# A transformer block with multi-query attention: another order of units, loads and evictions at the start of the kernel

## The chip, the cores and the metric

The kernel runs on one core of a Trainium2 chip, in one launch. The metric is device time in microseconds (us), from an execution of the whole program; lower is better. A core has TensorE (matmuls, written PE in the profile; its weight loads are PEld), VectorE (DVE), ScalarE (ACT), GpSimd (POOL) and SyncE (SP), which here issues nearly all DMAs. Each engine works through its own instructions in order and waits on semaphores for the others.

## The reference

The input x has 2048 tokens of 1024 elements. A condition vector c gives six vectors of 1024 (shift, scale and gate for attention; the same for the FFN). Queries have 32 heads of 32 elements; all heads share one key and one value head.

```python
mod = (silu(c) @ w_mod).reshape(1, 6, 1, -1)
sa, ca, ga, sb, cb, gb = mod[:, 0], ..., mod[:, 5]
h = layernorm(x) * (1 + ca) + sa
q = (h @ wq) -> 32 heads of 32;  k = h @ wk;  v = h @ wv        # one k and v for all heads
p = softmax(q k^T / sqrt(32))
x = x + ga * ((p v) @ wo)
h = layernorm(x) * (1 + cb) + sb
x = x + gb * ((silu(h @ w1) * (h @ w3)) @ w2)                   # F = 3584
```

All matrices are bf16, the output too.

## The kernel before, in words

**Tiling.** The 2048 tokens are eight blocks of 256 (NB, B). A block's attention is eight units of four heads (f = 0 to 7), and a unit goes through eight pairs of key tiles (NJ = 8, 256 keys each). One cycle is one pair of key tiles of one unit: eight S matmuls (K stationary, 32 rows of the array per head, four heads at once) fill four PSUM banks, two exponentials on ScalarE (each 128x1024) write one slot of the ring U, which has NU = 10 slots. After a unit's eight cycles come 64 matmuls with V (four heads at once by columns). The softmax denominator comes from VectorE adding the exponentials (`pairs`, `psum`) and a few matmuls of the sums with ones (`md_own`, or `md` for the later units, which are "merged"). VectorE divides and writes the result over the query tile in QT. In all there are 64 units, 512 cycles and 1024 exponentials.

When the eight units of block n are done, `after_attention(n)` runs: `wo` (output projection for both halves t of 128 tokens, the sum onto x, the second layer norm, and the transposition of the normalized rows to `h2t(n)`: by TensorE for blocks 0 and 7, by DMA for the others), `ffn1` (14 slabs of w1 and w3, each loaded by DMA) and `ffn2` (four quarters of w2). These matmuls (mode F in the code) fill TensorE between the S and V matmuls (modes S and A) of later blocks. After the last exponential only F work remains.

**The start.** SP issues the loads in the order of their due times: x tiles, the w_mod columns of scale (field 1) and shift (field 0), wq in two pieces. Each x tile (tt = 0 to 15) is normalized (`lnt1`: statistics on VectorE, root on GpSimd, the scaled copy on ScalarE for tt < 8 and on VectorE otherwise), transposed by TensorE and evicted to HT by ScalarE or VectorE. The scale is multiplied into wk, wv and wq; the shift enters as a bias: `mod_cols(0)` computes it as 64 narrow matmuls in a bank that it shares with the transposes, SAB holds it, `k_bias` makes the bias of the keys and of two query heads (QKB), `q_bias` that of the others, `v_setup` that of V. `k_proj(j)` makes a pair of key tiles (KT), `q_proj` the queries (QT) and `v_proj` V. The first exponential needs KT of pair 0, QT of unit 0 and so the shift. The queries of blocks 2 to 7 are projected during block 0; wq lies where the FFN's weight slots will be, and HT where the FFN's hidden tiles will be, so both must be done with before the FFN of block 0 can load its weights. `mod_chunk` computes the other four vectors during block 0; the attention gate is multiplied into wo (WOG).

**What sets the order.** Every operation is recorded by `op` with an engine, an estimated duration, the tiles that it reads and writes, and a due time vt. The class `Placer` then replays all of them on its own clock and picks, engine by engine, the next ready operation with the smallest due time plus an offset; S matmuls have by far the smallest due times (TOP). The offsets, and the slacks that say how long an engine may wait for a more urgent operation, stand in `PLAN`, one entry for each eight cycles (SPAN = 8), with an offset for each pair of tag and engine. The result is a fixed order for each engine, with the semaphore waits that it needs. Banks 6 and 7 of PSUM (PB in the profile) are lent to all operations but S; banks 0 to 5 belong to S. An operation with `alts` may go to either of two engines, whichever the planner finds earlier. All instructions are issued from one helper, so the profile has one line number (L22) for them and they are told apart by their tiles.

Names that matter below: `mod_cols` (line 1053), `k_proj` (1121), `v_proj` (1136), `q_proj` (1151), `s_exp` (1214), `sums` (1249), `av` (1312), `wo` (1378), and the loop over units at line 1596.

Of the kernel before, what the change touches and what calls it, by code (L numbers as in the profile page):

```python
# [8 lines left out]
P = 128  # L9
# [33 lines left out]
class Graph:  # L43
# [63 lines left out]
    def alias(self, new, old):  # L107
# [8 lines left out]
    (0.1, 0.03, 0.02, 0, 3.5,  # L116
     {"-/pe": -33, "-/act": 190, "-/dve": 5, "-/pool": 95, "-/sp": 76, "an/dve": -40, "av/dve": -55, "k/dve":
      91, "kb/pe": 35, "ln/pe": -95, "ln/act": 28, "ln/dve": 5, "ln/pool": 1, "mc/pe": 5, "mc/dve": 6, "mc/sp":
      -9, "mod/pe": -73, "mod/dve": 181, "out/sp": -53, "pair/dve": -76, "q/pe": 132, "q/sp": 35, "quarter/pe":
      -104, "quarter/dve": -1, "quarter/sp": 145, "s/pe": -277, "s/act": 37, "sc/dve": -253, "slab/pe": -4,  # L120
      "slab/dve": -34, "slab/sp": 86, "v/pe": 17, "v/dve": 37, "v/pool": 21, "wo/pe": -48, "wo/dve": 4,
      "wo/pool": -43, "wo/sp": -134}),
    (0.15, 0.1, 0.3, 0, 0.4,
     {"-/pe": -22, "-/pool": -69, "-/sp": -59, "an/dve": -5, "av/pe": -93, "av/dve": 169, "k/dve": 28, "kb/pe":
      15, "ln/pe": -116, "ln/dve": -52, "mc/pe": -6, "mc/dve": -14, "mc/sp": -13, "mod/pe": 4, "mod/dve": 88,
      "out/sp": -129, "pair/dve": 109, "q/pe": 17, "q/dve": -175, "quarter/pe": -52, "quarter/dve": 76,
      "quarter/sp": 24, "s/pe": -165, "s/act": -218, "sc/dve": -247, "slab/pe": -51, "slab/act": -199,
      "slab/dve": 23, "slab/sp": 201, "v/pe": -94, "v/dve": -54, "v/pool": 118, "wo/dve": 28, "wo/pool": 3,
      "wo/sp": 81}),
    (0.15, 0.12, 0.3, 1, 0.4,  # L130
     {"-/pe": 14, "-/act": 18, "-/pool": 26, "-/sp": 104, "an/dve": -18, "av/pe": 1, "av/dve": 110, "k/dve":
      118, "ln/pe": -18, "ln/act": 1, "ln/dve": -311, "ln/pool": 109, "mc/pe": 68, "mc/dve": 53, "mc/sp": 12,
      "mod/pe": 78, "out/sp": 258, "pair/dve": -12, "q/pe": 54, "q/dve": -107, "q/sp": -43, "quarter/pe": -71,
# [671 lines left out]
def build(nc, x_in, wq_in, wk_in, wv_in, wo_in, w1_in, w3_in, w2_in, c_in, wmod_in, out, S, D, F):  # L805
# [4 lines left out]
    B = 256  # L810
# [16 lines left out]

# [834 lines left out]
```

## Time and profile before

| | us |
|---|---|
| median of 3 runs | 1135.16 (1134.17 to 1136.1) |
| the profiled execution, time | 1133.24 |
| its span, first to last instruction | 1131.4 |
| ScalarE busy in it | 1019.8 |
| of that, 1024 exponentials | 963.4 |
| VectorE busy | 990.1 |
| mean granted clock of TensorE | 0.995 of full speed |

A row of the stretches gives the stretch, its length, the busy time of each engine with the number of its instructions in brackets, the granted clock, the share of the DMA engines and the GB/s that they moved. A row in order of time gives start, length, engine, operation, output <- input, and how many equal instructions in a row were merged; in square brackets the engine's idle time before it and what ended it. A busy TensorE is not TensorE at its peak: matmuls overlap, and their ends are modelled. "S" as an output is one of the six S banks, "PB" one of the two others; "HT,W" as inputs is a projection or an FFN matmul, "U,V" attention's second product, "PS,ONES" the denominators.

### The profile page before, as it was taken

How to read it: one execution, taken by the hardware profiler on the slowest of the kernel's cores; microseconds unless marked ns; L12 is line 12 of the kernel's file. 1: busy time of each engine (PE TensorE's matmuls, PEld its weight loads, DVE VectorE, ACT ScalarE, POOL GpSimd, SP SyncE). 2: the span in 40 equal slices, each digit the busy share in tenths (PEclk: the TensorE clock that was granted, in tenths of full speed). 3: DMA queues.
4: the chain of work that ended last, by engine and by line, in shares of the span. 5: the costliest groups of instructions: out<-in, count | busy, mean ns of one | idle time of the engine just before them, and what ended most of it. 6: DMA issues, size and time to landing. Idle time of an engine off the chain costs nothing.

```text
span 1131.4 us, 34236 instructions
## 1 busy us (share of the span) xinstructions
PE 1105.2 (98%) x15344; PEld 751.9 (66%) x15376; DVE 990.1 (88%) x1492; ACT 1019.8 (90%) x1161; POOL 55.8 (5%) x95
## 2 busy tenths in 40 slices
PE   8999998999999999999999999999999999999998
PEld 6644445666567766776667766776577757776887
DVE  8989999988899989998899889998999889987542
ACT  6999999999999999999999999999999999984110
POOL 5100000000100001000100001000100001000000
PEclk9999998999999999999999999999999999999999
DMA  9500378655596657965697576775597567677793
GB/s 343 185 2 2 113 205 227 186 169 160 141 248 195 194 146 181 241 196 144 150 270 197 160 192 179 228 197 154 135 264 205 160 174 207 191 220 216 220 295 112
DMA packets 374290, 209.43 MB, mean 185 GB/s; under 512 B 17536, under 2 KB 365952, under 8 KB 374144
## 3 DMA queue, kind: packets, MB, share of 16 engines
q1 hardware_dynamic: 373712, 207.11, 65.8%
q8 instruction: 121, 1.98, 0.8%
q14 instruction: 25, 0.20, 0.1%
q10 hardware_dynamic: 432, 0.13, 0.0%
HBM read 199.89 MB, written 4.19 MB: 180 GB/s over the span
## 4 chain that ended last, share of the span: by engine, by line
ACT 51%; PE 36%; DVE 10%; POOL 1%; issue 1%; POOLq 0%; DVEq 0%
ACT U L22 47%; PE PB L22 23%; PE S L22 13%; ACT HT L22 4%; DVE PS L22 4%; DVE ST L22 2%; DVE X L22 1%; POOL RS L22 1%; DVE QT L22 1%; DVE XNB L22 1%; DVE RB L22 1%; DVE MV L22 0%; DVE HT L22 0%; ACT XNB L22 0%; DVE RC L22 0%
## 5 line engine op out<-in xcount | busy, mean ns | idle before, releaser
L22 ACT ACTIVATE U<-S 128x1024 bf16<-128x1024 f32 x1024 | 963.4, 1170 | 4.6 <-PE S L22 2.6
L22 DVE TENSOR_TENSOR PS<-U 128x2048 bf16<-128x2048 bf16 x256 | 310.2, 1219 | 34.4 <-ACT U L22 31.0
L22 DVE TENSOR_TENSOR PS<-PS 128x1024 bf16<-128x1024 bf16 x312 | 274.5, 882 | 5.0
L22 PE MATMUL PB<-QT,W 128*128 128x256 bf16 x1824 | 228.3, 273 | 1.0
L22 PE MATMUL S<-QT,KT 32*128 32x256 bf16 x4096 | 204.2, 273 | 9.0 <-ACT U L22 5.7
L22 PEld LDWEIGHTS PB<-QT,W 128*128 128x128 bf16 x1824 | 166.4, 98 | 49.8 <-issue 29.2
L22 PE MATMUL PB<-W2S,HT 128*128 128x256 bf16 x1540 | 190.4, 273 | 0.0
L22 PEld LDWEIGHTS PB<-W2S,HT 128*128 128x128 bf16 x1540 | 141.0, 98 | 39.6 <-issue 23.2
L22 PEld LDWEIGHTS S<-QT,KT 32*128 32x128 bf16 x4096 | 60.8, 92 | 139.4 <-ACT U L22 129.7
L22 PE MATMUL PB<-U,V 128*32 128x256 bf16 x4096 | 127.9, 274 | 0.0
L22 PE MATMUL PB<-QT,HT 128*128 128x256 bf16 x928 | 117.8, 273 | 0.7
L22 PEld LDWEIGHTS PB<-U,V 128*32 128x32 bf16 x4096 | 106.5, 97 | 11.1 <-issue 6.1
L22 PE MATMUL PB<-HT,W 128*128 128x256 bf16 (+1 forms) x560 | 98.7, 316 | 3.1 <-issue 2.4
L22 PEld LDWEIGHTS PB<-QT,HT 128*128 128x128 bf16 x928 | 84.8, 98 | 25.4 <-issue 15.1
L22 ACT ACTIVATE HT<-PB 128x512 bf16<-128x512 f32 (+1 forms) x103 | 74.1, 719 | 10.9 <-PE PB L22 10.8
L22 DVE TENSOR_TENSOR HT<-HT,PB 128x512 bf16<-128x512 bf16 x100 | 68.3, 683 | 9.1 <-PE PB L22 7.2
L22 DVE SCALAR_TENSOR_TENSOR HT<-HT,PB 128x512 bf16<-128x512 bf16 x100 | 68.1, 681 | 7.7 <-ACT HT L22 7.1
L22 PEld LDWEIGHTS PB<-HT,W 128*128 128x128 bf16 x576 | 50.0, 97 | 37.0 <-issue 14.9
L22 ACT ACTIVATE HT<-S 128x512 bf16<-128x512 f32 (+1 forms) x16 | 11.1, 702 | 59.9 <-PE S L22 59.9
L22 POOL TENSOR_SCALAR RS<-MV 128x1 f32<-128x1 f32 x32 | 10.5, 327 | 967.9 <-DVE MV L22 966.4
L22 PE MATMUL PB<-WO,QT 128*128 128x512 bf16 x209 | 51.4, 380 | 2.3 <-issue 2.1
L22 PEld LDWEIGHTS PB<-WO,QT 128*128 128x128 bf16 x224 | 18.9, 97 | 25.3 <-issue 6.3
(112 smaller groups left out, 691.8 us busy)
## 6 DMA issues: line engine op xcount, KB each, us to landing
W<-in_B_w_dram SPq DMA_DIRECT2D x150, 512.0 KB, 4.9
W2S<-in_B_w_dram SPq DMA_DIRECT2D x28, 1792.0 KB, 8.5
HT<-in_B_w_dram SPq DMA_DIRECT2D x74, 512.0 KB, 5.0
W2S<-in_w_mod_dram SPq DMA_DIRECT2D x8, 1024.0 KB, 6.9
X<-in_A_x_dram SPq DMA_DIRECT2D x8, 512.0 KB, 6.9
out_dram<-X SPq DMA_DIRECT2D x7, 512.0 KB, 7.8
U<-in_B_w_dram SPq DMA_DIRECT2D x1, 3584.0 KB, 18.2
W2S<-in_B_w_dram SPq DMA_DIRECT2D x1, 3584.0 KB, 13.7
```

What stands on the lines that cost most here:

```text
L22: return getattr(e, call[0])(*call[1], **call[2])
```

## The change

1. Units 0 and 1 (block 0, f = 0 and 1) take turns in halves of the keys: unit 0 with pairs 0 to 3, unit 1 with 0 to 3, unit 0 with 4 to 7, unit 1 with 4 to 7 (`CYC`). After each half, `half` runs V and ones matmuls into one bank, side by side; the first half's bank is copied to PT (f32), the second's added to it. VectorE's `pairs` and `psum` fall away for these two units.
2. The other units of block 0 are two f, that is eight heads, by 128 queries (`UN`): first f 2+3, 4+5, 6+7 with queries 0 to 127, then the same with 128 to 255. QT's dependencies are kept by halves t, and `wo` is split by t; `wo(0, 0)` is recorded after unit 4.
3. The shift's w_mod columns are loaded ahead of x tiles 8 to 11, which become two loads; wq's second piece goes last. `mod_cols(0)` writes to bank 2 instead of a lent bank.
4. Evictions of HT for tiles 10 to 15 and of KT for pairs 2 to 7 have VectorE alone (EVA, EVK). V is projected earlier (VV), and the queries f = 2 to 7 of blocks 0 and 1 are due by pairs.
5. A few estimated durations are changed, and all offsets of `PLAN` are others (66 entries before, 66 after, one of them the same). The instructions of blocks 1 to 7 are the same, their order is not.

```diff
-    (0.1, 0.03, 0.02, 0, 3.5,
-     {"-/pe": -33, "-/act": 190, "-/dve": 5, "-/pool": 95, "-/sp": 76, "an/dve": -40, "av/dve": -55, "k/dve":
...
+    (0.15, 0.06, 0.0, 1, 2.5,
+     {"-/pe": -103, "-/act": -50, "-/sp": 3, "an/dve": 282, "av/dve": -1, "k/pe": -256, "k/dve": -10, "kb/pe":
...
-    LV = {}
+    HALVES = (0, 1)
+    WO00 = 10
+    EVA = 10
+    EVK = 2
+    VV = (-1576, -1575, -1530, -1480)
...
+    PT = [PS[:, k].rearrange("p h q -> p (h q)").bitcast(F32) for k in (1, 3)]
...
-    x_dma(8, 4, -1893)
-    wm_dma(0, 0, -1892)
+    wm_dma(0, 0, -1893)
+    x_dma(8, 2, -1892)
     wm_dma(0, 1, -1891)
-    wq_dma(2, NC, "WQ1", -1890)
+    x_dma(10, 2, -1890)
     x_dma(12, 4, -1889)
+    wq_dma(2, NC, "WQ1", -1888)
...
-        op("act", ev_a, 0.92, reads=bk, writes=hk, vt=vt, sess=s, alts=[("dve", ev_d, 0.6)])
+        if tt < EVA:
+            op("act", ev_a, 0.92, reads=bk, writes=hk, vt=vt, sess=s, alts=[("dve", ev_d, 0.6)])
+        else:
+            op("dve", ev_d, 0.6, reads=bk, writes=hk, vt=vt, sess=s)
 
     def mod_cols(fld):
         G.tag = "mod"
-        s = Sess()
+        s = Sess() if fld else None
+        bk = [] if fld else [("S", 2)]
...
+               writes=[("mod", fld)] + bk, vt=-1800, mode="F", sess=s, post=0.145)
...
+           alts=[] if j >= EVK else [("act", lambda b=0: [lambda e: e.activation(KT[:, ts], BANK[b][:, 0:256], ACT.Identity,
...
+    UN = [(0, f, 1, 0) for f in HALVES] + [(0, f, 2, t) for t in range(2) for f in range(len(HALVES), NC, 2)]
+    UN += [(n, f, 1, 0) for n in range(1, NB) for f in range(NC)]
+    CYC = [(u, q) for a in range(2) for u in HALVES for q in range(4 * a, 4 * a + 4)]
+    CYC += [(u, q) for u in range(len(HALVES), NB * NC) for q in range(NJ)]
+    CIX = {uq: c for c, uq in enumerate(CYC)}
+
+    def qt(u, g=None):
+        n, f, nf, t = UN[u]
+        ps = slice(0, P) if g is None else slice(32 * g, 32 * (g + 1))
+        return QT[ps, n, f:f + nf, t * P:t * P + B // nf]
+
+    def qk(u):
+        n, f, nf, t = UN[u]
+        return [("QT", n, f + k, t + m) for k in range(nf) for m in range(2 // nf)]
+
+    def v3(ap, u):
+        return ap.rearrange("p (a b) -> p a b", a=UN[u][2])
+
...
+    def half(u, a):
+        G.tag = "av"
+        s = Sess(False)
+        t = PT[u]
+        qs = range(4 * a, 4 * a + 4)
+        for q in qs:
+            def mm(b, q=q):
+                return [lambda e, h=h, kk=kk, w=w, c=c: e.matmul(
+                    BANK[b][32 * h:32 * (h + 1), c:c + B], w, U[:, CIX[u, q] % NU, h, kk, :],
+                    start=(q == qs[0] and kk == 0 and c == 0), stop=(q == qs[-1] and kk == 1),
+                    tile_position=(0, 32 * h), skip_group_check=True)
+                    for kk in range(2) for w, c in ((V[:, 2 * q + kk, :], 0), (ONES[:, 0:32], B)) for h in range(4)]
+            op("pe", mm, 0.4368, reads=["ONES", ("V", q // 2), ("U", CIX[u, q] % NU, 0), ("U", CIX[u, q] % NU, 1)],
+               writes=[("av", u)], vt=-500 + u, mode="A", sess=s, post=0.145, after=[exps[(CIX[u, qs[-1]], 1)]])
+        G.tag = "an"
+        if a == 0:
+            op("dve", lambda b: [lambda e: e.tensor_copy(t, BANK[b])], 0.6, reads=[("av", u)], writes=[("PT", u)],
+               vt=u * 8.0, sess=s)
+            return
+        op("dve", lambda b: [lambda e: e.tensor_tensor(t, t, BANK[b], ALU.add)], 0.62, reads=[("av", u), ("PT", u)],
+           writes=[("PT", u)], vt=u * 8.0, sess=s)
+        op("dve", lambda: [lambda e: e.transpose(RB[:, 0, :], t[:, B:2 * B])], 0.37, reads=[("PT", u)],
+           writes=["RBD"], vt=u * 8.0)
+        finish_av(u, t[:, 0:B], ("PT", u))
...
-    def wo(n, vt):
...
+    def wo(n, t, vt):
         G.tag = "wo"
-        for t in range(2):
...
+    def norm2(n, vt):
+        G.tag = "wo"
         if 0 < n < NB - 1:
...
-                o.bw = 200e3
+                o.bw = 185e3
...
-        v_proj(tb, -1150 + tb)
+        v_proj(tb, VV[tb])
...
-        q_proj(0, 2, f, 8.0 * f - 30)
+        q_proj(0, 2, f, 8.0 * (f // 2) - 22)
...
-        wo(n, e0 - 30)
+        for t in range(2):
+            if n or t:
+                wo(n, t, e0 - 30)
+        norm2(n, e0 - 30)
...
-    for u in range(NB * NC):
-        for j in range(NJ):
-            s_exp(NJ * u + j)
+    for c, (u, q) in enumerate(CYC):
+        s_exp(c)
+        if u in HALVES:
+            if q % 4 == 3:
+                half(u, q // 4)
+            if q == 7:
+                G.alias([("PS", (1, 3)[u])], [("PT", u)])
+            continue
+        if q < NJ - 1:
+            continue
         av(u)
-        done = [v for v in ((u - 1, u) if not merged(u) else (u - 1,)) if v % NC == NC - 1 and v >= 0 and
-                (v == u) != merged(v)]
-        for v in done:
-            after_attention(v // NC)
+        if u == 4:
+            wo(0, 0, WO00)
+        if not merged(u) and u % NC == NC - 1:
+            after_attention(u // NC)
+        elif u and merged(u - 1) and u % NC == 0:
+            after_attention(u // NC - 1)
     last = 64 * NB - 1
     later = []
```

More of the change, by code (lines that the diff above doesn't have):

```diff
@@ L1250, in sums @@
         if u < MERGE0:
-            lev = LV.get(u, 2)
-            for q in range(0, NP, 2) if lev else ():
-                pairs(u * NJ + q, q)
+            for q in range(0, NP, 2):
+                pairs(CIX[u, q], q)
                 G.tag = "av"
-                if lev > 1:
-                    psum(q, q, q + 1, u * NJ + q + 102.0)
-            return list(range(0, NP, lev)) if lev else []
+                psum(q, q, q + 1, u * NJ + q + 102.0)
+            return list(range(0, NP, 2))
         acc = 4 + u % 2
@@ L1368, in h2t, with h2k @@
         return H20 if n == 0 else QT[:, n - 1, :, :]
-    def h2k(n):
-        return [("H20", cc) for cc in range(NC)] if n == 0 else [("QT", n - 1, cc) for cc in range(NC)]
+    def h2k(n, cs=range(8)):
+        return [("H20", cc, t) if n == 0 else ("QT", n - 1, cc, t) for cc in cs for t in range(2)]
     def xk(n, t, qs=range(4)):
```

977 lines of the change are left out of this document (491 added, 486 removed).

## The prediction, made before the change was run

> **What bounds the kernel now.** I read the page first (busy shares), then busy time in stretches, then the chain of waits, and last the instructions in order of time where the stretches show idle engines.
>
> ```profile
> span 1131.4 us, 34236 instructions
> PE 1105.2 (98%) x15344; PEld 751.9 (66%) x15376; DVE 990.1 (88%) x1492; ACT 1019.8 (90%) x1161; POOL 55.8 (5%) x95
> ...
> core 0: us, PE busy (x) PEld busy (x) DVE busy (x) ACT busy (x) POOL busy (x), PEclk, DMA share, GB/s
> 0.00:10.00 10.00, 8.46 (x70) 6.27 (x70) 5.26 (x13) 4.08 (x5) 2.98 (x14) 1.00 0.82 286
> 10.00:20.00 10.00, 8.48 (x130) 6.68 (x128) 9.72 (x25) 8.86 (x9) 6.54 (x15) 0.83 1.07 371
> 20.00:30.00 10.00, 7.96 (x156) 6.87 (x154) 9.73 (x23) 5.80 (x6) 6.16 (x15) 0.99 1.06 380
> ...
> 40.00:152.00 112.00, 107.42 (x1627) 52.22 (x1646) 103.44 (x173) 112.00 (x124) 0.79 (x2) 1.00 0.16 50
> 152.00:185.00 33.00, 27.70 (x500) 14.54 (x504) 30.11 (x57) 31.54 (x35) 4.59 (x4) 0.90 0.92 248
> 185.00:1000.00 815.00, 807.32 (x11370) 551.74 (x11380) 755.09 (x1077) 811.60 (x928) 30.59 (x36) 1.00 0.70 189
> ...
> 1040.00:1080.00 40.00, 40.00 (x346) 33.06 (x345) 19.70 (x36) 4.18 (x7) 1.59 (x4) 1.00 0.88 249
> ```
>
> Four stages. Up to 30 us the kernel loads and normalizes x; VectorE is 97% busy from 10 us on, and ScalarE has not begun its exponentials. From 40 to 152 us (attention of block 0) ScalarE is busy all 112 us: it sets the pace. From 152 to 185 us ScalarE goes on, but TensorE has only 27.70 us of 33: it has run out of other work and waits for block 0's second layer norm. From 185 us to 1000 us TensorE (99.1%) and ScalarE (99.6%) are tied, and the tail after 1040 us is TensorE alone at 100%. So the end is TensorE's total work plus its idle time, and nearly all of that lies ahead of 185 us. The change works there.
>
> **Step 1: the exponentials begin sooner.** ScalarE, then TensorE and VectorE, in order of time:
>
> ```profile
> 25.06 1.75 PE L22 MATMUL PB<-SCC,U 128*128 128x16 bf16 x64
> ...
> 27.58 0.14 DVE L22 CAST SAB<-PB 128x8 bf16<-128x8 f32 x1
> ...
> 28.00 0.54 PE L22 MATMUL PB<-SAB,W 128*128 128x16 bf16 x16
> ...
> 29.15 0.10 DVE L22 COPY QKB<-PB 128x3 f32<-128x3 f32 x1
> ...
> 30.29 0.40 PE L22 MATMUL S<-QT,KT 32*128 32x256 bf16 x8
> ```
> ```profile
> 30.76 3.76 ACT L22 ACTIVATE U<-S 128x1024 bf16<-128x1024 f32 x4
> 34.38 0.96 ACT L22 ACTIVATE KT<-PB,QKB 128x256 bf16<-128x256 f32 x2
> 35.39 1.02 ACT L22 ACTIVATE U<-S 128x1024 bf16<-128x1024 f32 x1
> 36.35 0.47 ACT L22 ACTIVATE KT<-PB,QKB 128x256 bf16<-128x256 f32 x1
> 36.73 1.01 ACT L22 ACTIVATE U<-S 128x1024 bf16<-128x1024 f32 x1
> 37.63 0.48 ACT L22 ACTIVATE KT<-PB,QKB 128x256 bf16<-128x256 f32 x1
> 38.11 1.02 ACT L22 ACTIVATE HT<-PB 128x1024 bf16<-128x1024 bf16 x1
> 39.03 31.29 ACT L22 ACTIVATE U<-S 128x1024 bf16<-128x1024 f32 x34
> ```
>
> The first exponential at 30.76 us is the end of a chain from the shift: its 64 narrow matmuls at 25.06, SAB, the biases QKB, keys and queries, S. The three rates of the load stage give (286+371) x 10 = 6.57 MB by 20 us. Queued up to the end of the shift are, by the code, 8 x tiles (2.10 MB), two fields of w_mod (4.19), the first wq columns (0.52), x tiles 8 to 11 (1.05) and wk, wv (0.13): 7.99 MB, through at 20 + 1.42/0.38 = 23.7 us. After the change half of tiles 8 to 11 stand behind it: 0.52/0.38 = 1.4 us sooner. Splitting that load is one more issue on SP's queue, which stands ahead of the engines' needs and costs no transfer time. Second, the shift's sum now has a bank of its own, so its first 48 matmuls run when the first part is in, and 16 remain: 1.75 x 48/64 = 1.3 us off the chain. Third, SAB came 0.77 us after the matmuls' end and QKB 0.6 us after its own: VectorE's queue was busy. That need not change; I count 0.7 of these 1.4 us as won. Sum 3.4 us; bounds 1.4 (DMA alone) and 5.7 (25.06 to 30.76, the whole chain).
>
> **Step 2: ScalarE spared.** After 30.76 us it does four key evictions and one of HT, 0.96+0.47+0.48+1.02 = 2.93 us. Evictions of keys 2 to 7 and of tiles 10 to 15 now go to VectorE alone. Because the exponentials begin 3.4 us sooner, one HT eviction of tiles below 10 that stood ahead of them may fall among them (1.02 us). So 1.9 us; bounds 0.9 and 2.9. The price moves to VectorE:
>
> ```profile
> 43.16 0.69 DVE L22 COPY HT<-PB 128x1024 bf16<-128x1024 bf16 x1
> ...
> 45.19 0.48 DVE L22 TENSOR_SCALAR KT<-PB,QKB 128x256 bf16<-128x256 f32 x1 [0.32 <-PE PB L22]
> ...
> 49.60 1.49 PE L22 MATMUL PB<-U,V 128*32 128x256 bf16 x48
> ...
> 50.11 2.35 DVE L22 TENSOR_TENSOR PS<-U 128x2048 bf16<-128x2048 bf16 x2
> ...
> 53.84 0.68 DVE L22 TENSOR_TENSOR PS<-PS 128x1024 bf16<-128x1024 bf16 x1
> ...
> 56.61 0.75 DVE L22 TENSOR_SCALAR QT<-PB,QKB 128x512 bf16<-128x512 f32 x1 [0.22 <-PE PB L22]
> ...
> 57.90 0.62 PE L22 MATMUL PB<-PS,ONES 128*32 128x256 bf16 x16
> ```
>
> Four keys at 0.48 and one tile at 0.69 are 2.6 us more for VectorE ahead of its last key, which it wrote at 45.19 to 45.67: now 48.3 at worst. The halves cover this: units 0 and 1 take keys 0 to 3 first, and keys 4 to 7 are asked for from the ninth pair of key tiles on. A pair is two exponentials, 2 x 31.29/34 = 1.84 us, so key 7 is needed 11 pairs, 20.2 us, after the start. With a start at 27.4 us that is 47.6 us, less than a microsecond short in the worst case. Without the halves key 7 would be due at 27.4 + 12.9 = 40.3 us and ScalarE would stand 8 us.
>
> VectorE also loses work: units 0 and 1 no longer sum their exponentials (eight additions of 1.18 and eight of 0.68, 14.9 us); two copies and additions of a 512-wide bank come instead (a sum from PSUM of that size, "X<-X,PB" below, took 0.69: 2.8 us). TensorE pays: 64 ones matmuls per unit beside the 64 of V, at 1.49/48 = 0.031 us, less the 0.62 us that the old denominator took: 2 x (2.0-0.6) = 2.8 us.
>
> What can be late next is unit 2, which now needs two heads' queries at once. ScalarE's stream behaves as if it had begun at 39.03 - 6 x 0.92 = 33.5 us; with steps 1 and 2 that is 28.2, and unit 2 starts 16 pairs (29.4 us) later, at 57.6. The second wide query eviction ended at 57.4. wq's rest now lands last, 1.05 MB or 2.8 us later, and TensorE has the ones on top. Unit 2 and those behind it (S stands in TensorE's order, so everything queued there waits) may lose 0 to 2.8 us; I take 1.0. Block 0's exponentials then end 3.4+1.9-1.0 = 4.3 us sooner.
>
> **Step 3: half of the output projection moves ahead.** The end of block 0's attention, all engines in order of time:
>
> ```profile
> 158.33 0.43 DVE L22 TENSOR_TENSOR QT<-RB 128x256 bf16<-128x256 f32 x1
> ...
> 161.47 1.47 PE L22 MATMUL PB<-WO,QT 128*128 128x512 bf16 x6
> ...
> 164.26 0.68 DVE L22 TENSOR_TENSOR X<-X,PB 128x512 bf16<-128x512 bf16 x1
> ...
> 171.28 0.69 DVE L22 TENSOR_TENSOR X<-X,PB 128x512 bf16<-128x512 bf16 x1
> ...
> 178.40 2.63 DVE L22 TENSOR_SCALAR HT<-PB,MODC 128x256 bf16<-128x256 bf16 x8
> ...
> 184.74 0.39 PE L22 MATMUL PB<-HT,W 128*128 128x256 bf16 x2
> ```
>
> From the last head (158.76) to the FFN's first matmul (184.74) are 26 us, in which TensorE gets 32 projection matmuls, six per pair. With units of eight heads by 128 queries, the first half's heads are complete after unit 4, so 16 matmuls, two additions and its norm run inside block 0, and only 16 follow the last unit. The second half's first addition can then stand where the first half's second stood: 171.28 becomes about 165.3, 6.0 us sooner. Bounds: 0, if weights or modulation are what is waited for; 7.0, all between 164.26 and 171.28. The half that moves (16 x 0.245 = 3.9 us by 1.47/6) lands in a stretch where TensorE has 4.6 of 112 us idle; it and the ones displace some query projections past 152 us, into the 5.3 idle us there.
>
> **Sum.** FFN of block 0 starts 4.3+6.0 = 10.3 us sooner, but 6.0/1.84 = 3.3 pairs are then still undone, each S (0.40) and eight matmuls of V (8 x 0.031 = 0.25): -2.1. Of the 2.8 us of ones I let 1.0 find no idle time (bounds 0 and 2.8). Net 7.2. The profiled execution took 1133.24 us, 1.84 around its span and 1.92 under the median of 1135.16. So 1126.0 beside it, 1128 beside the median. Were ScalarE alone the limit up to 1031 us, the 4.3 us would remain; with every bound at its better end it is 15.6 less 3.8 x 0.65, 13 us.
>
> **The searched order** touches the 815 us too. The same chain of waits once per block:
>
> ```profile
> 444.38 4.58 ACT U L22 x5
> ...
> 569.51 4.58 ACT U L22 x5
> ```
>
> 125.1 us a block. With both engines over 99% little is to be won (0.9% of 815 is 7 us at most); I take 0, and the rival prices a loss.
>
> **Rivals.** (A) the forecast, 1128, own range 1124 to 1132: 0.50. (B) As A, and the clock stays up:
>
> ```profile
> 175.00:180.00 5.00, 2.65 (x34) 1.55 (x32) 4.54 (x10) 4.46 (x6) 1.17 (x1) 0.71 1.17 305
> 180.00:185.00 5.00, 4.58 (x86) 2.47 (x86) 3.52 (x7) 4.07 (x6) 0.00 (x0) 0.61 1.19 290
> ```
>
> The granted clock falls to 0.71 and 0.61 just where TensorE starved, and ScalarE lost 0.54+0.93 us to late S. If the shorter wait avoids that, 1.5 us more: 1126.5; against it, the norm's chain itself stays: 0.12. [...] (C) Something else holds the FFN's start (weights go where wq and HT lay, so every query projection must be done first): step 3 gives nothing, 4.3-1.0 = 3.3 us, 1132: 0.15. (D) Slower: the order fits the long stage worse. It decides from 1.2 us a block on (7.2/6 blocks); at 1.5% of 125.1 us, 1.9 us x 6 = 11.3, less 7.2, 1139. For it: the tie, where either engine's stall counts. Against: unchanged instructions there, and 8 us of 815 idle now: 0.16. (E) It doesn't start sooner: VectorE, 97% busy, brings keys and queries later by its own 2.6 us and wq's 2.8, which eats the 5.3 of steps 1 and 2, and unit 2 loses its full 2.8: 6.0-2.1-1.0-2.8 = 0.1, 1135: 0.07.
>
> **Numbers.** 0.2% (2.3 us) is about what can be told from no change here. Faster takes A, B and most of C: 0.75; same, parts of C, D and E: 0.09; slower: 0.16. The range 1121 to 1138 holds A, B, C, E.
>
> **What would show it.** First exponential near 27.4 us; no key or HT evictions on ScalarE after the first few; the exponentials without gaps through unit 2; FFN's first matmul near 174.4 us with the projection's first half before 120 us; block period 125.1. A gap at unit 2, a FFN start above 180, or a period above 126 would make it wrong.

## The result, and the profile after

The changed kernel took 1131.39 us (median of 8 runs, 1130.23 to 1132.69); the kernel before took 1134.7 beside it (8 runs). The ratio is 0.9969 [0.9958, 0.998]: 3.3 us faster where 7.2 had been forecast. Its profiled execution took 1131.4 us, with a span (first to last instruction) of 1129.6. From the end of the last exponential to the end of the span both kernels take the same, 100.35 us before and 100.38 after (from 1031.10 and 1029.22 us on), and every trace below shows 100.35 to 100.40: what the change gains comes through ScalarE's stream of exponentials.

The page of the changed kernel, and its stretches in the columns of the prediction:

```profile
PE 1110.8 (98%) x15472; PEld 753.3 (67%) x15472; DVE 976.4 (86%) x1484; ACT 1017.2 (90%) x1155; POOL 51.5 (5%) x95
```
```profile
10.00:20.00 10.00, 7.26 (x131) 5.87 (x130) 9.02 (x24) 8.91 (x9) 6.49 (x14) 1.00 1.07 371
20.00:30.00 10.00, 9.09 (x157) 7.46 (x155) 8.26 (x21) 5.69 (x6) 5.08 (x13) 1.00 1.05 381
30.00:40.00 10.00, 9.09 (x190) 7.06 (x189) 10.00 (x25) 8.27 (x9) 2.91 (x7) 1.00 0.71 241
...
152.00:185.00 33.00, 29.93 (x494) 14.42 (x495) 31.18 (x58) 33.00 (x37) 2.77 (x4) 1.00 0.66 175
185.00:1000.00 815.00, 811.37 (x11411) 554.17 (x11404) 756.18 (x1083) 811.30 (x928) 27.76 (x36) 1.00 0.71 191
```

The kernel before, from 30 to 40 us:

```profile
30.00:40.00 10.00, 9.77 (x156) 7.12 (x153) 8.93 (x19) 9.55 (x14) 2.56 (x7) 1.00 0.96 341
```

Three things are to be seen. ScalarE is less busy than before from 30 to 40 us (8.27 against 9.55), so waits and not exponentials have taken the place of its evictions, and VectorE is busy in all of it (10.00 against 8.93). The granted clock of TensorE is 1.00 where it was 0.83 (10 to 20 us) and 0.90 (152 to 185). And TensorE seems to have gained 5.6 us of work. That last one needs care: before, 15344 matmuls stand beside 15376 weight loads, so at least 32 records are missing. An experiment below with the changed kernel's matmuls reads 1105.6 us with 34 records fewer, so missing records alone can be worth 5 us. The same holds for the "8 us of idle time" that the prediction read from the 815 us: 11370 records there before, 11411 now.

ScalarE in order of time; it can be held against the second fence of the prediction's step 1:

```profile
30.51 5.61 ACT L22 ACTIVATE U<-S 128x1024 bf16<-128x1024 f32 x6 [1.96 <-PE S L22]
36.83 1.94 ACT L22 ACTIVATE U<-S 128x1024 bf16<-128x1024 f32 x2 [0.72 <-PE S L22]
39.27 5.61 ACT L22 ACTIVATE U<-S 128x1024 bf16<-128x1024 f32 x6 [0.50 <-PE S L22]
45.11 1.94 ACT L22 ACTIVATE U<-S 128x1024 bf16<-128x1024 f32 x2 [0.24 <-PE S L22]
47.30 14.77 ACT L22 ACTIVATE U<-S 128x1024 bf16<-128x1024 f32 x16 [0.25 <-PE S L22]
```

The first exponential comes at 30.51 us in place of 30.76, not at 27.4. The evictions between exponentials are replaced by waits for S (0.72 + 0.50 + 0.24 + 0.25 = 1.71 us). Counted as the prediction did, the gap-free stream behaves as if it had begun at 47.30 - 16 x 0.92 = 32.6 us; it was 33.5, and 28.2 was forecast.

Around the FFN's start, all engines of the changed kernel in order of time:

```profile
178.78 1.47 PE L22 MATMUL PB<-HT,W 128*128 128x512 bf16 x6
...
180.27 4.91 SPq L22 DMA_DIRECT2D W<-in_B_w_dram  x4
...
181.42 2.64 DVE L22 TENSOR_SCALAR HT<-PB,MODC 128x256 bf16<-128x256 bf16 x8
...
185.48 0.39 PE L22 MATMUL PB<-HT,W 128*128 128x256 bf16 x2
```

The first half's projection runs at 157 us, about where it ran before, not ahead of 120. The last query projection ends at 180.25, and the weights that take wq's place are asked for 0.02 us later. The 4.91 us of that row are the issuing of four loads on SP's queue; the first of them lands 5.0 us after its issue, at about 185.3. The scaled evictions of the second norm end at 184.06. The FFN starts at 185.48 (184.74 before).

**The clock.** The kernel before, then the changed one, in stretches of 3.41 us (the clock is the third column from the end):

```profile
16.68:20.09 3.41, 3.41 (x22) 2.67 (x21) 3.38 (x10) 2.63 (x3) 2.36 (x4) 0.50 1.06 389
...
173.71:177.12 3.41, 1.50 (x26) 0.78 (x27) 2.95 (x10) 3.41 (x5) 1.99 (x2) 1.00 0.77 210
177.12:180.54 3.42, 2.29 (x30) 1.25 (x27) 3.42 (x9) 2.88 (x4) 0.00 (x0) 0.50 1.19 290
```
```profile
126.25:129.66 3.41, 2.63 (x88) 2.13 (x84) 3.41 (x11) 3.41 (x5) 0.00 (x0) 1.00 0.05 13
129.66:133.07 3.41, 3.41 (x26) 1.24 (x19) 2.45 (x7) 2.60 (x4) 0.00 (x0) 0.50 0.84 278
```

The mean clocks of the prediction's rows (0.71, 0.61) are whole windows of 3.41 us at half clock (177.12 to 183.95). The window ahead of them shows TensorE busy for 1.50 us by its records, the one ahead of 16.68 for 1.89, the one ahead of the changed kernel's 129.66 for 2.63. Before has three half-clock windows in its profiled execution, the changed kernel one, at another place. ScalarE, the kernel before and then the changed one, shows what such a window costs:

```profile
179.04 3.77 ACT L22 ACTIVATE U<-S 128x1024 bf16<-128x1024 f32 x4 [0.54 <-PE S L22]
183.74 3.77 ACT L22 ACTIVATE U<-S 128x1024 bf16<-128x1024 f32 x4 [0.93 <-PE S L22]
```
```profile
132.76 1.94 ACT L22 ACTIVATE U<-S 128x1024 bf16<-128x1024 f32 x2 [0.81 <-PE S L22]
135.12 53.35 ACT L22 ACTIVATE U<-S 128x1024 bf16<-128x1024 f32 x58 [0.41 <-PE S L22]
```

Two windows cost before 0.54 + 0.93 = 1.47 us of late S, one costs the changed kernel 0.81 + 0.41 = 1.22. Between 48 us and the first HT eviction behind (187.38 and 188.37 us) there are no others; an experiment's trace without a window (new_start_old_rest below) has none from 63 to 187 us. A half-clock window takes half of its 3.41 us, 1.71, of TensorE's time, 0.15% of the span, so by this estimate a run's mean clock tells how many it had: 1.000 none, 0.998 one, 0.997 two, 0.995 three, 0.994 four, 0.992 five, 0.991 six. The traces in which none, one, two, three and five windows were seen have these means. Mean spans by that number (runs in brackets; those of before stood beside the experiments):

| windows | 0 | 1 | 2 | 3 | 4 | 5 | 6 |
|---|---|---|---|---|---|---|---|
| before | | | 1132.9 (1) | 1132.6 (24) | 1133.4 (19) | 1134.3 (32) | 1134.9 (2) |
| changed | 1128.6 (3) | 1130.0 (4) | 1130.9 (1) | | | | |

Before has 4.1 windows on average, the changed kernel 0.75. A window costs before about 0.85 us ((1134.3-1132.6)/2) and the changed kernel 1.4.

### The profile page after: what moved, and what is told of

Its sections match the earlier page's. It is cut to its first block, busy times and chain, and to the rows that moved or that the text cites. A ratio compares the mean times of both kernels' runs of the same rounds, so it can differ in the third digit from the quotient of the medians.

```text
span 1129.6 us, 34462 instructions
## 1 busy us (share of the span) xinstructions
PE 1110.8 (98%) x15472; PEld 753.3 (67%) x15472; DVE 976.4 (86%) x1484; ACT 1017.2 (90%) x1155; POOL 51.5 (5%) x95
## 4 chain that ended last, share of the span: by engine, by line
PE 73%; ACT 22%; DVE 2%; DMA 1%; issue 0%; SPq 0%; POOL 0%
PE PB L22 55%; ACT U L22 21%; PE S L22 19%; DMA W<-in_A_wq_dram 1%; ACT HT L22 1%; DVE ST L22 1%; DVE PS L22 1%; DVE HT L22 0%; SPq L22 0%; ACT XNB L22 0%; DVE KT L22 0%; DVE XNB L22 0%; POOL RS L22 0%; DVE QT L22 0%; DVE X L22 0%
## 5 line engine op out<-in xcount | busy, mean ns | idle before, releaser
L22 DVE TENSOR_TENSOR PS<-U 128x2048 bf16<-128x2048 bf16 x248 | 300.9, 1218 | 34.1 <-ACT U L22 30.9
L22 DVE TENSOR_TENSOR PS<-PS 128x1024 bf16<-128x1024 bf16 x304 | 268.3, 883 | 4.8
L22 PE MATMUL PB<-W2S,HT 128*128 128x256 bf16 x1512 | 187.5, 273 | 0.0
L22 PEld LDWEIGHTS PB<-W2S,HT 128*128 128x128 bf16 x1512 | 138.2, 98 | 39.4 <-issue 23.6
L22 PE MATMUL PB<-U,V 128*32 128x256 bf16 x4096 | 132.3, 273 | 0.6 <-DVE QT L22 0.6
L22 PE MATMUL PB<-HT,W 128*128 128x256 bf16 (+1 forms) x576 | 103.3, 320 | 1.1 <-DVE QT L22 0.5
L22 ACT ACTIVATE HT<-PB 128x512 bf16<-128x512 f32 (+1 forms) x102 | 71.4, 701 | 9.0 <-PE PB L22 8.2
L22 POOL TENSOR_SCALAR RS<-MV 128x1 f32<-128x1 f32 x32 | 14.2, 445 | 968.8 <-DVE MV L22 968.8
L22 PE MATMUL PB<-WO,QT 128*128 128x512 bf16 x224 | 55.4, 381 | 0.0
```

Of the source, the lines that this page charges most:

```text
L22: return getattr(e, call[0])(*call[1], **call[2])
```

## The experiments

In all of them the order of the instructions is a written list that takes the place of the planner's search.

**Which half of the kernel pays.** Everything up to about 250 us from one kernel, the order of the rest from the other:

```diff
- SEQ = changed[0:end]
+ SEQ = before[0:250 us] + changed[250 us:end]      (old_start_new_rest)
+ SEQ = changed[0:250 us] + before[250 us:end]      (new_start_old_rest)
```

> The kernel before up to about 250 us (its units, its order), then the changed kernel's order of the same remaining work. Theory 'the gain lies in the order behind block 0' (after 185 us TensorE's idle time fell from 7.7 to 3.6 us): as fast as the changed kernel, 1131 to 1132 us, ratio to before 0.997. Rival 'the gain comes from block 0 (units in turns, shift, evictions) and from what block 0 hands over at 185 us': no gain, 1134 to 1135 us.

Measured: 1133.54 us, ratio 0.9987 [0.9978, 0.9996].

> The changed kernel up to about 250 us, then the order of before for the same remaining work. Theory 'order behind block 0': no gain left, 1134 to 1135 us. Rival 'block 0': as fast as the changed kernel, 1131 to 1132 us. If both halves pay, each of the two runs lies about half way, 1133.

Measured: 1132.74 us, ratio 0.9979 [0.997, 0.9988]. Both halves pay, as the second expectation's last sentence has it. By windows the two come apart:

| windows | 0 | 1 | 3 | 4 | 5 |
|---|---|---|---|---|---|
| old start, new rest | | | 1131.5 (7) | 1132.3 (1) | 1133.6 (3) |
| new start, old rest | 1130.7 (6) | 1132.0 (5) | | | |

The old start brings three to five windows, the new one none or one. At equal windows the new order of the rest gains 2.1 us with the new start (1130.7 to 1128.6 without windows, 1132.0 to 1130.0 with one), but 1.1 us with the old start at three windows (1132.6 to 1131.5) and 0.7 at five (1134.3 to 1133.6). The traces show why. From the start of the 257th exponential (at 274 to 281 us) to the end of the last one, the old order takes 754.50 us before and 754.82 with the new start, the new order 753.51 with either start (753.51 to 753.55 in the traces below, but for norm_late's 753.81; before_kept_busy, in the old order, has 755.86). So the order itself gains at least 1.0 us. The rest of the 2.1 is lost at the joint of the new start with the old rest, where ScalarE waits as it does in neither kernel:

```profile
260.72 1.02 ACT L22 ACTIVATE U<-S 128x1024 bf16<-128x1024 f32 x1 [0.82 <-PE S L22]
```

The line of before, carried on to none, 1132.6 - 3 x 0.85 = 1130.0, lies below the new start's 1130.7, of which some 0.8 us are the joint's. So whether the new block 0 gains anything beside the clock is not shown; no run of before had fewer than two windows, and the line's end is an estimate. The idle times of 7.7 and 3.6 us on which the first expectation leans are the missing records spoken of above.

**The evictions back on ScalarE.**

```diff
-    EVA = 10
-    EVK = 2
+    EVA = 16
+    EVK = 8
```

In the list, key pairs 2 to 5 and tile 13 then carry ScalarE as their engine.

> The changed kernel in its own order, but the evictions of key pairs 2 to 5 and of tile 13 are done by ScalarE, as before. Prediction's step 2 (ScalarE sets the pace, 2.9 us of evictions delay every later exponential): 1.9 to 2.9 us slower than the changed kernel, 1133.3 to 1134.3 us. Rival 'VectorE, busy 100% from 30 to 40 us, is what the keys wait for, and ScalarE stands 1.7 us for S there anyway': within 1 us of the changed kernel either way, 1130.5 to 1132.4 us, with ScalarE's waits for S between 30 and 48 us shorter by what it now evicts.

Measured: 1131.9 us, ratio 0.9967 [0.9954, 0.9979], against 0.9969 for the changed kernel; 1130.4 with one window (3 runs) against 1130.0. ScalarE's row of the gap-free stream, behind evictions of keys at 35.87 and 40.83 and of HT at 42.99, and the page's busy times:

```profile
43.90 18.62 ACT L22 ACTIVATE U<-S 128x1024 bf16<-128x1024 f32 x20
```
```profile
PE 1105.6 (98%) x15438; PEld 752.8 (67%) x15472; DVE 974.4 (86%) x1479; ACT 1019.5 (90%) x1160; POOL 51.6 (5%) x95
```

The gap-free stream begins at 43.90 us with 12 exponentials done, as if at 32.9 (32.6 in the changed kernel). What ScalarE evicts, it had waited for S anyway: the rival holds, and its waits for S between 30 and 48 us fall from 1.71 to 0.80 us.

**The loads in the old order.**

```diff
- WM0[0,0], X8-9, WM0[0,1], X10-11, X12-15, WQ1
+ X8-9, X10-11, WM0[0,0], WM0[0,1], WQ1, X12-15
```

> The changed kernel with the loads in the order of before: x tiles 8 to 11 ahead of the shift's columns, the rest of wq ahead of x tiles 12 to 15; all engine orders unchanged. Prediction's step 1 (1.4 us of the first exponential's gain is the shift's earlier load): first exponential about 1.4 us later, total 1.4 us slower, 1132.8 us. Rival 'the shift's last 16 matmuls stand in TensorE's queue behind a transposition that waits for ScalarE, so the load was not the last to come': first exponential moves by less than 0.5 us and the total stays within 0.7 us of 1131.4.

Measured: 1132.88 us, ratio 0.9975 [0.9966, 0.9984]; 1130.7 with one window (5 runs) and 1131.3 with two (4). So 0.4 to 0.7 us at equal windows, and 1.6 windows on average in place of 0.75. Its profiled execution, TensorE and ScalarE in order of time, and the stretches:

```profile
24.92 1.36 PE L22 MATMUL S<-SCC,U 128*128 128x16 bf16 x48 [1.95 <-DMA U<-in_w_mod_dram]
...
34.73 5.61 ACT L22 ACTIVATE U<-S 128x1024 bf16<-128x1024 f32 x6 [3.27 <-PE S L22]
```
```profile
23.05:26.46 3.41, 1.54 (x52) 1.51 (x53) 1.89 (x5) 2.37 (x2) 1.82 (x5) 1.00 1.05 375
26.46:29.87 3.41, 3.06 (x56) 2.94 (x54) 0.85 (x4) 2.05 (x2) 0.47 (x2) 0.50 1.06 381
```

Both expectations missed on the first exponential. The total is the one's 1132.8 by the medians (1.5 us above the changed kernel), but the ratios are only 0.0006 x 1135 = 0.7 us apart, the end of the other's range. TensorE waits 1.95 us for the shift, that window is thin, and two windows at half clock follow (26.46 to 33.29 us); the first exponential comes 4.2 us later, not 1.4 or under 0.5. Yet the end loses only about a microsecond, and more than half of that by the windows. Loading the shift sooner matters, mostly by way of the clock, and most of what happens to the first exponential does not arrive at the end.

**The first exponential alone.**

```diff
  PE order, from 24 us:
- IDENT,XNB(7)  SCC,U(last 16)  SAB,PS  SAB,W  K1  K2  K3  S(0)
+ SCC,U(last 16)  IDENT,XNB(7)  SAB,PS  SAB,W  K2  S(0)  K1  S(1)  K3
```

VectorE's order changes with it: biases, first keys and first queries stand ahead of the statistics of later tiles.

> The changed kernel; only the order of some 30 instructions between 24 and 33 us differs: the shift's last matmuls ahead of tile 7's transpositions, then biases, first keys, first queries and the first S at once, one key projection ahead of it in place of three. Prediction's step 1 (what the first exponential gains, the end gains while ScalarE sets the pace): first exponential at 28.3 in place of 30.5 us, 1.4 to 2.2 us faster than the changed kernel, ratio to before 0.995 to 0.996. Rival 'VectorE, without an idle moment from 30 to 40 us, sets when the keys and the second unit's queries come': the exponentials start at 28.3 us and then stand for it, the gap-free stream begins no sooner, and the total is the same or up to 2.5 us slower, ratio 0.997 to 0.999.

Measured: 1133.12 us, ratio 0.9978 [0.9969, 0.9987]; 1130.4 without windows (5 runs), 1.8 us slower than the changed kernel. ScalarE, and the stretch ahead of 30 us:

```profile
28.35 1.94 ACT L22 ACTIVATE U<-S 128x1024 bf16<-128x1024 f32 x2
...
38.71 1.94 ACT L22 ACTIVATE U<-S 128x1024 bf16<-128x1024 f32 x2 [4.08 <-PE S L22]
...
49.19 13.86 ACT L22 ACTIVATE U<-S 128x1024 bf16<-128x1024 f32 x15 [0.25 <-PE S L22]
```
```profile
20.00:30.00 10.00, 8.68 (x157) 6.94 (x154) 6.26 (x17) 7.34 (x8) 4.39 (x11) 1.00 1.05 382
```

The exponentials begin 2.2 us sooner and then stand 4.08 us. The gap-free stream begins at 49.19 with 16 done, 1.9 us later than in the changed kernel, and the end is 1.8 us later. The end follows the gap-free stream, not its first instruction. VectorE, from which the later keys and queries come, is busy 6.26 us from 20 to 30 where it was busy 8.26: it now waits for TensorE 1.51 us at 26.70 and 0.78 us at 29.43 instead of going on with the statistics, and with 9.96 of the 10 us from 30 to 40 it can't make that up. Those 2.0 us are the size of the stream's delay. So a sooner first exponential that is paid for with VectorE's time is a loss; what one without that price would bring, this run does not show.

**Fewer ones matmuls.** The first two units take their denominators from two of the eight key pairs.

```diff
-                    for kk in range(2) for w, c in ((V[:, 2 * q + kk, :], 0), (ONES[:, 0:32], B)) for h in range(4)]
+                    for kk in range(2) for w, c in ((V[:, 2 * q + kk, :], 0), (ONES[:, 0:32], B))[:1 + (q == qs[-1])] for h in range(4)]
```

> The changed kernel in its own order; the denominators of the first two units are taken from two of the eight key pairs only (other output), so 96 of their 128 ones matmuls are gone, 96 x 0.031 = 3.0 us of TensorE's work before 80 us. Prediction's step 2 (some 1 of 2.8 us of ones finds no idle time): 0.7 to 1.0 us faster than the changed kernel. Rival 'TensorE is not the limit in block 0, its work there only fills time between two S': no difference, ratio to before 0.997; FFN's first matmul within 0.5 us of 185.5 (184.4 at full clock).

Measured: 1130.72 us, ratio 0.9957 [0.9945, 0.997]; 1127.9 without windows (2 runs) and 1129.2 with one (3), 0.7 and 0.8 us less than the changed kernel. The two profiled executions, with one window each, are only 0.2 us apart (spans of 1129.4 and 1129.6), and the FFN's first matmul comes at 185.28, as the rival said. So the prediction's price for the ones, 1.0 us, is of the right size, but few runs stand behind it.

**The projection's first half moved ahead.**

```diff
  PE order, 95 to 188 us:
- q(4,6) mc0 ... mc1 mc2 q(4,7) mct1 q(6,0) q(6,1) ... q(6,4) ... wo(0,0) ... q(6,5) wo(0,1) q(6,6) q(6,7)
+ q(4,6) mc0 ... mc1 ... mct1 ... wo(0,0) q(6,..) ... q(6,5) wo(0,1) q(6,6) q(6,7)
```

> The changed kernel's instructions in another order between 95 and 188 us: wo's scaling by the gate and the first half's 16 projection matmuls run 15 us sooner, right behind the scaling (about 139 to 144 us in place of 157 to 167); query projections and the second units' sums fill what they leave behind. Prediction's step 3 (the second half's first addition stands where the first half's second stood, FFN 6 us sooner): FFN's first matmul at 179 us, total 4 to 6 us faster than the changed kernel, ratio to before 0.992 to 0.994. Rival 'the second half waits for the last unit's heads at 159 us and for its norm, and the FFN's weights for the last query projection; what moves ahead only changes places with query projections': FFN's first matmul between 184 and 188 us, total the same as the changed kernel or up to 2.5 us slower, ratio 0.997 to 0.999.

Measured: 1131.85 us, ratio 0.9975 [0.9966, 0.9984]; 1129.7 without windows (6 runs), 1.1 us slower than the changed kernel; the rival's range. TensorE, and the stretch ahead of the FFN's start:

```profile
139.76 0.81 PE L22 MATMUL PB<-WO,QT 128*128 128x512 bf16 x3 [0.16 <-DVE WO L22]
...
186.54 0.39 PE L22 MATMUL PB<-HT,W 128*128 128x256 bf16 x2
```
```profile
182.78:186.19 3.41, 3.41 (x68) 2.04 (x63) 2.13 (x5) 2.27 (x3) 0.00 (x0) 0.50 1.00 288
```

The 16 matmuls did move ahead, to 140 us, and query projections fill the place that they left. The second half's two additions come at 167.97 and 172.86 us in place of 169.64 and 174.20, so 1.3 to 1.7 us sooner and not 6; the last query projection ends 1.3 us sooner (178.97). But VectorE has sums and query evictions to do ahead of the norm's scaled evictions, which end only 0.3 us sooner (183.78). The FFN starts at 186.54, not at 179, and a half-clock window lies right ahead of it in this execution. Why the runs without windows are slower than the changed kernel stays open.

**The last query projections cut.**

```diff
-                BANK[b][:, 0:w], ...
+                BANK[b][:, 0:(32 if n == 6 and f > 4 else w)], ...
-                HT[:, cc, ts],
+                HT[:, cc, n * B:n * B + (32 if n == 6 and f > 4 else w)],
```

> The changed kernel in its own order; the last three query projections ahead of the FFN (24 matmuls for token blocks 6 and 7, heads 20 to 31) compute 32 of their 512 columns (other output), so about 24 x 0.22 = 5 us of TensorE's work between 164 and 180 us is left out and w1 and w3 can be loaded sooner. Rival C of the prediction (the FFN's start is held by the query projections and the weights that take wq's place): FFN's first matmul 2 to 5 us sooner, at 180.5 to 183.5 us, total 2 to 5 us faster than the changed kernel, ratio to before 0.993 to 0.995. Theory 'the second norm's own chain ends at 184.1 us, just ahead of the weights': FFN's first matmul no more than 2.2 us sooner (what the projection's second half gains by the first of the three), total 0 to 2 us faster, ratio 0.9955 to 0.997.

Measured: 1131.66 us, ratio 0.9972 [0.9961, 0.9983]: 5 us of work gone and no gain. Its stretches, and its FFN's start:

```profile
171.57:174.98 3.41, 1.77 (x27) 0.61 (x26) 2.99 (x6) 3.41 (x5) 0.00 (x0) 1.00 0.70 173
174.98:178.40 3.42, 1.73 (x24) 0.64 (x24) 3.28 (x5) 3.42 (x5) 1.11 (x2) 0.50 0.00 0
```
```profile
184.37 0.39 PE L22 MATMUL PB<-HT,W 128*128 128x256 bf16 x2
```

Two windows at half clock follow the thin one, and all seven runs have two or three. With two they take 1128.8 us (2 runs) against 1130.9 (1 run) of the changed kernel: the work was worth some 2 us, going by that one run, and the clock took them. The ratio lies just above both ranges. The FFN starts 1.1 us sooner, which is within the theory's 2.2. The first weights are now asked for at 177.81 us and land 3.9 us later, 2.7 us ahead of the FFN's first matmul, so they no longer hold it. The norm's scaled evictions end at 183.00, and the FFN follows 1.37 us behind (184.06 and 1.42 us in the changed kernel), right after 40 matmuls with V that stand ahead of it in TensorE's order.

**TensorE kept busy.** Matmuls of no use, 512 columns each, into a bank that the next matmul overwrites:

```diff
+            [lambda e: e.matmul(BANK[b], ONES[:], WMB[r][:, 0, :], start=True, stop=True)] * {7: 2}.get(i, 0) +
...
+            [lambda e: e.matmul(BANK[b], ONES[:], XNB[:, 1, 0:4 * P], start=True, stop=True)] * {6: 3, 7: 4}.get(i, 0) +
```

> The kernel before, with nine more 512-wide matmuls (0.22 us each, about 2 us of work) written to banks that the following matmuls overwrite: three ahead of the last gate's first ones product (171.1 us), two ahead of the last modulation chunk (172.5), four ahead of its ones product (174.7), all where TensorE stood idle. Theory 'the half clock from 177.1 to 183.9 us, which follows TensorE's thin stretch from 171 to 177, is what the changed block 0 avoids': the clock stays at 1.00 there (or falls for one window of 3.4 us instead of two) and the kernel is 1 to 2 us faster than before although it does more work, ratio 0.998 to 0.999. Rival 'the clock costs nothing, since ScalarE waits for its own chain there': ratio 1.000 to 1.002.

Measured: 1134.7 us, ratio 0.9995 [0.9986, 1.0003], between the two ranges; 1.9 windows on average in place of 4.1. Its one run without any has a span of 1130.7.

> The kernel before up to about 250 us with the nine filling matmuls of before_kept_busy, then the changed kernel's order of the rest. Theory 'block 0's new units gain only by keeping TensorE's clock up, and the order behind them gains 2 us': in runs whose granted clock is 1.000 the span is that of the changed kernel at that clock, 1128.4 to 1129.0 us; since the fillers spare only one of two windows in most runs, the median lies at 1131.5 to 1133 us, ratio to before 0.997 to 0.998. Rival 'the new units gain by themselves too': spans at a clock of 1.000 of 1130.5 us and more, ratio 0.9987 as the old start with the new rest had without fillers.

Measured: 1133.96 us, ratio 0.9986 [0.9977, 0.9995], 2.3 windows in place of 3.6. The rival's number, though no run was free of windows to test its claim. In both the fillers spare windows but cost time: with three windows 1133.3 us (3 runs) against 1132.6 of before, and 1132.3 (5) against 1131.5, about 0.8 us. So they show that a little work in the right place raised the clock here, not that the clock is all that block 0 gained.

> The changed kernel, with five more 512-wide matmuls (0.22 us each): three ahead of the first gate's ones product (126.3 us), two ahead of the second modulation chunk (127.8), ahead of the half clock that the profiled execution shows from 129.7 to 133.1 us. Theory 'clock': every run at a granted clock of 1.000, 1.1 us faster than the changed kernel's profiled execution, ratio to before 0.996. Rival 'the drop costs nothing': ratio 0.997 as the changed kernel has, or above it.

With `{1: 2}` and `{0: 3}` in the changed kernel: 1130.8 us, ratio 0.996 [0.9947, 0.9972], four of five runs without windows. By the ratio it is 1 us below the changed kernel, by the medians 0.6, and the intervals overlap. Its runs without windows are no faster than those of the changed kernel (1129.0 against 1128.6): what it gains can only be the windows spared.

**What the new order of the rest gains.** In the kernel before GpSimd's power for block 3's second norm takes 1.53 us, beside a sum of exponentials on VectorE; in the changed kernel 0.57. One line of VectorE's order, in four blocks:

```diff
  DVE order:
- MV  COPY(av)  STREAM_TRANSPOSE  RECIPROCAL  XNB  STREAM_TRANSPOSE  QT  PS<-U
+ MV  PS<-U  COPY(av)  STREAM_TRANSPOSE  RECIPROCAL  XNB  STREAM_TRANSPOSE  QT
```

> The changed kernel; in four of the six blocks behind block 0 one VectorE sum of exponentials (1.22 us) stands right behind the second norm's mean and variance, as in the old order, in place of four instructions later. Theory 'the new order gains behind block 0 because GpSimd's power (0.57 us beside copies from PSUM, 1.53 us beside such a sum) and VectorE's normalization come about 1 us sooner, so that the FFN's first matmuls no longer catch up with their scaled inputs': GpSimd's power takes 1.5 us again in these four blocks, normalization 1 us later, each block 0.3 to 0.5 us longer, 1.2 to 2 us in all, ratio to before 0.998 to 0.9987. Rival 'TensorE is busy there without a gap, so the norm has slack': no change, ratio 0.997.

Measured: 1130.79 us, ratio 0.996 [0.9947, 0.9972]; 1128.7 without windows (3 runs), the changed kernel has 1128.6. In order of time the kernel before, the changed one, and this one:

```profile
557.90 0.21 DVE L22 BATCH_NORM_AGGREGATE MV<-ST 128x2 f32<-128x12 f32 x1
558.83 1.53 POOL L22 TENSOR_TENSOR RS<-RS,NH 128x1 f32<-128x1 f32 x1
560.39 0.55 DVE L22 TENSOR_SCALAR XNB<-X,MV,RS 128x1024 bf16<-128x1024 bf16 x1
```
```profile
558.05 0.21 DVE L22 BATCH_NORM_AGGREGATE MV<-ST 128x2 f32<-128x12 f32 x1
558.66 0.57 POOL L22 TENSOR_TENSOR RS<-RS,NH 128x1 f32<-128x1 f32 x1
559.37 0.50 DVE L22 TENSOR_SCALAR XNB<-X,MV,RS 128x1024 bf16<-128x1024 bf16 x1
```
```profile
557.05 0.21 DVE L22 BATCH_NORM_AGGREGATE MV<-ST 128x2 f32<-128x12 f32 x1
557.18 1.17 DVE L22 TENSOR_TENSOR PS<-U 128x2048 bf16<-128x2048 bf16 x1
557.36 1.07 POOL L22 TENSOR_SCALAR RS<-MV 128x1 f32<-128x1 f32 x1 [2.17 <-DVE MV L22]
558.51 0.57 POOL L22 TENSOR_TENSOR RS<-RS,NH 128x1 f32<-128x1 f32 x1
559.20 0.50 DVE L22 TENSOR_SCALAR XNB<-X,MV,RS 128x1024 bf16<-128x1024 bf16 x1
```

From MV to XNB it takes 2.49, 1.32 and 2.15 us. GpSimd's power did not take 1.5 us again: the sum was over before it. The instruction ahead of it on GpSimd stands beside the sum now and takes 1.07 us, where it took 0.23 in the changed kernel (at 558.35), so the norm is late all the same. A norm that comes 0.83 us later in four blocks costs next to nothing, 0.3 us in the stretch from the 257th exponential to the last one (753.81 against 753.51) and not 1.2 to 2, so my theory falls as stated. ScalarE's waits from 190 to 1035 us (in total, how many, the longest), of the kernel before, then of the changed one:

```profile
ACT HT L22 <- PE PB L22: 3.3, 7, 1.3
ACT U L22 <- PE S L22: 1.1, 6, 0.2
```
```profile
ACT HT L22 <- PE PB L22: 2.4, 1, 2.4
```

Before has six short waits for the FFN's products (0.33 us each, one per block) and six for S, which are gone but for one of 0.2 us; in the last block its wait of 1.3 us has become one of 2.4. Another wait of 1.6 us, in the last block too, is in both. The waits shrink from 6.0 to 4.2 us. Whether they are the gain or its sign, and what in the order removes them, stays open.

## Why the prediction was right or wrong

**Faster, by the wrong road.** The sign was right and 1131.4 lies in the range; the forecast was 3.4 us too low, and none of its three steps brought what it was to bring. That the time fell into the range is luck, since most of what was gained had been priced at nothing or held unlikely. By the prediction's own signs it was wrong: the first exponential came at 30.51 us and not near 27.4, and the FFN's start at 185.48 lies above 180. Rival C's time, 1132, is the nearest, but its sum is 4.3 us of steps 1 and 2, which did not come either.

**Step 1 (3.4 us)** failed at what it took for its end. The split load did not slow the queue (371 and 381 GB/s from 10 to 30 us, 371 and 380 before), and the shift did come sooner: with the old load order the first exponential is 4.2 us later, and the bias QKB comes at 27.89 us in place of 29.15. But the new order puts the shift's last 16 matmuls behind a transposition that waits for ScalarE, and three key projections ahead of the first S. TensorE of the changed kernel:

```profile
25.06 0.62 PE L22 MATMUL PB<-IDENT,XNB 128*128 128x128 bf16 x8 [0.40 <-ACT XNB L22]
25.52 0.55 PE L22 MATMUL S<-SCC,U 128*128 128x16 bf16 x16
...
27.02 3.11 PE L22 MATMUL PB<-HT,PS 128*128 128x256 bf16 x24
30.06 0.40 PE L22 MATMUL S<-QT,KT 32*128 32x256 bf16 x8
```

So of the 1.26 us that QKB gained the first exponential kept 0.25. And first_exp_sooner shows that 2.2 us gained there at VectorE's cost are lost again: the stream from its last gap on is what counts, and VectorE's work sets when that is. The stream gained 0.9 us where steps 1 and 2 said 5.3. Rival E had this mechanism (VectorE brings keys and queries late) at 0.07.

**Step 2 (1.9 us)** failed in the same place: evictions taken from ScalarE became waits for S of 1.71 us. Its worry about unit 2 was not needed, since from 47.30 us the exponentials run without a gap until the half-clock window at 130. Its price for the ones, 1.0 us, was of the right size: 0.7 and 0.8 at equal windows, 0.2 between two traces.

**Step 3 (6.0 us)** failed twice. The order found left the first half at 157 us; before 120 it could not have been, since the gate is multiplied into wo only from 134.58 to 140.79 us. And moved ahead by force it brings the second half 1.3 to 1.7 us, not 6, and the norm's end 0.3, because the query projections fill its place on TensorE and VectorE's other work stands ahead of the norm's evictions. Rival C's gate is there, but not alone: the weights are asked for 0.02 us behind the last query projection and land 0.2 us ahead of the FFN, yet with the queries cut and the weights there 2.7 us early the FFN gained only 1.1 us, since the second norm's evictions and attention's matmuls ended no sooner than that.

**Rival B, the clock (1.5 us, chance 0.12)** is, by the following estimate, the larger part of what came. Mean spans are 1133.6 us before (the 78 runs beside the experiments) and 1129.6 after. A straight line through the runs of before has 1130.2 at no windows and 0.81 us for each, through those of the changed kernel 1128.6 and 1.24. So 4.13 x 0.81 - 0.75 x 1.24 = 2.4 us come from windows and 1130.2 - 1128.6 = 1.6 from the rest. The line's value at none is an extrapolation, with a standard error of 0.3 us. In the changed kernel's profiled execution the windows were avoided near the second norm, as the rival said, and in the load stage (16.68 to 20.09), which it did not see. The windows lie on a grid of 3.41 us: before, the half clock sets in at 16.68 and at 177.12 us, 47.0 windows apart, and in old_start_new_rest at 27.92 and 178.10, 44.0 apart. The windows ahead of a drop that stand in this text show TensorE busy for 1.50 to 2.63 us of 3.41. Why the clock falls behind these and not behind others is not shown.

**The searched order (0 us)** gained 1.0 us from the 257th exponential to the last one (754.50 to 753.51), the opposite of rival D. "Little is to be won" rested on rows with both engines above 99%, and 0.13% of 755 us is already 1 us. Of the 1.6 us beside the windows that leaves 0.6 for block 0, which is not clear of the line's error.

## What to carry to other kernels

Where TensorE is near its limit, count the half-clock windows of every run before explaining a difference of microseconds, and look for the thin stretch ahead of each: a few matmuls of no use may be cheaper than the window (here 1128.9 against 1129.6 us in the mean, not clear of the noise), and work taken away may bring some (here two or three in all seven runs of late_queries_out). What is gained at the head of a stream counts only from the last gap of that stream on. Work moved ahead on an engine that is full pushes something else back; ask what the next stage waits for among that. Where two orders are joined for an experiment, look at the joint before the difference is put down to either.

## What the runs showed of the hardware that was not expected

In these traces TensorE's half clock came in whole windows of 3.41 us on a grid that ran through the execution (47.0 windows from 16.68 to 177.12 us before), one to three in a row (three from 178.10 to 188.34 us in old_start_new_rest), and cost 0.8 to 1.4 us of the span each by the estimates above. A stretch of 16-column matmuls and short waits, 126.25 to 129.66 us in the changed kernel, 2.63 of 3.41 us busy by its records, was followed by a half-clock window in one execution, and three of the eight executions of this kernel had none at all. Busy time alone does not tell: 13.60 to 17.01 us of the same execution, on the same grid, shows only 1.98 us, and no half clock follows. What decides stays open.

GpSimd's power of 128x1 took 0.57 us beside VectorE's copies from PSUM and 1.53 us when VectorE had begun a sum of 2048-wide bf16 pairs from SBUF ahead of it (558.70 to 559.92 us). The scaling ahead of the power took 0.23 us, and 1.07 beside such a sum: begun 0.18 us behind the sum, it ended 0.08 us behind it. So the two GpSimd instructions took 0.96 and 0.84 us more beside such a sum; by what means is not shown.
